# Who issues two small loads, who builds a table, and a new written order for all five queues

## The chip, the cores and the metric

One core of one Trainium2 chip runs the whole program. The metric is the device time of one execution in microseconds (us), given as the median over runs. A profile of one further execution supplies the rows that are quoted.

## The reference: what is computed

Sequence length S = 2048, width D = 448, hidden width F = 1792, all tensors bfloat16. Cut to what matters:

```python
def _A_ref(q, k, v, shift_k, ssm_k, ssm_D):      # q is layernorm(x)
    # k_shift[s] = sum over t of k[s-3+t] * shift_k[:, 3-t]      (4 taps per channel)
    kv = k_shift * v
    # y = causal convolution of kv with ssm_k, length 2048, per channel, by FFT of 4096 points
    y = y + kv * ssm_D
    return q * y

def _B_ref(x, w1, b1, w2, b2):                   # mixes tokens
    h = layernorm(x)
    u = gelu(einsum("bsd,sf->bdf", h, w1) + b1)
    return (einsum("bdf,fs->bds", u, w2) + b2) transposed to (b, s, d)

x = A_q
h = x + _A_ref(layernorm(x), A_k, A_v, A_shift_k, A_ssm_k, A_ssm_D)
h2 = h + _B_ref(layernorm(h), B_w1, B_b1, B_w2, B_b2)
```

## The kernel before

The 2048 positions are held as 128 partitions times R = 16 rows (position = 16 q + r). The long convolution is a transform built from matmuls in two stages, a product in the frequency domain, and two inverse stages. The program is a list of small operations, each with a step name "tag.number" and a position in that step, so `k2.5:4` is operation 4 of step 5 of tag k2. The tags, in the order of the data:

- `dummy`: a memset of a scratch tile by VectorE (L1061), a ScalarE activation that loads the GELU table (L1062), and nine matmuls on the scratch tile (L1071) that occupy TensorE until data is there.
- `con`: constants. `con.0` is the identity (L866, tensor c_id), `con.1` the first-stage table, `con.2` a compact second-stage table FC (c_fw, 258 KB). `con.3` to `con.6` spread FC into the full table FW, four operations on all of 1024 elements per partition (L881 on ScalarE, L882 on VectorE); every matmul of the second stage reads FW. `con.7` to `con.12` are later tables.
- `loads`: `loads.0` zeroes the fourth quarter of the filter tile KN (L903, VectorE); `loads.1` to `loads.4` load the four quarters of `ssm_k` (L906); `loads.5` loads the four taps `shift_k` in three pieces (L909 and two of L912); `loads.6, 7, 9, 11` are k and `loads.8, 10, 12, 13` v, in quarters of the rows; the rest are small vectors. The load of the fourth KN quarter, `loads.4`, has to wait for the memset `loads.0`.
- `kT`: transposes of the filter (L1083), evacuated to SBUF by ScalarE (L801) or VectorE (L804).
- `kv`: transposes of k (L986), a block of tap diagonals built by GpSimd (`kv.0`, L966 and L971), the four-tap convolution as matmuls (L1012), and the multiplication by v straight out of PSUM on VectorE (L1051).
- `k1` and `u1`: first transform stage of the filter and of kv (L1110, L1115), evacuated by either engine (L1126), then shuffled by DMA from SBUF to SBUF (L1130).
- `k2` and `u2`: second stage (L1150); the filter's is scaled on evacuation (L802, L805), the other copied (L801, L804).
- `i1`: 16 products in the frequency domain (L1176, 1792 elements per partition, all on VectorE), matmuls of the first inverse stage (L1195, 64 for each of eight groups), two evacuations for each group (L801) and two shuffling DMAs (L1210, L1215). `i1.4` is the group jj = 1, `i1.16` the group jj = 7.
- `q` and `xn`: layernorm statistics of x (L1252, L1254 on VectorE; the power on GpSimd, L1263) and normalised rows (L1285).
- `i2`: second inverse stage, row by row (L1316, L1321), gating by the normalised x (L1330, L1351, L1340), statistics of the result (L1357, L1369 and the small L1360, L1392) and the normalised row Q (L1402). `zero` is a GpSimd memset (L1161). `warm` are filler matmuls (L1226).
- `mlp`: the token MLP: 16 rows times 7 matmuls (L1449), 7 times 16 (L1459) with GELU, then 16 rows of output (L1470), each finished by VectorE (L1473) and stored.

Nothing is scheduled on the chip. The dictionary `ORDER` writes out, for each of the five queues (TensorE "pe", ScalarE "act", VectorE "dve", GpSimd "pool", SyncE "sp"), every operation in the order in which it is issued, and thereby also the engine of each operation that may run on more than one. A queue is strictly in order: an operation that waits holds back all that stand behind it. A planner in `schedule` walks these lists with estimated durations (`est`, `lat`, `rate`, `late`). It settles only which PSUM banks and buffers are taken, and so which waits are emitted. PSUM has eight banks; an evacuation of 896 elements frees a pair of them.

Apart from one output store on ScalarE's queue, all DMAs are issued by SyncE. The evacuations of k1, u1, k2, u2 and i1 alternate between ScalarE and VectorE as the lists say.

Of the kernel before, what the change touches and what calls it, by code (L numbers as in the profile page):

```python
# [33 lines left out]
    ),  # L34
    "act": (
# [9 lines left out]
    ),  # L45
    "dve": (
# [13 lines left out]
    ),  # L60
    "pool": (
        "kv.0:1-2 loads.14:0 q.0:0-1 kv.0:0 kv.0:3 q.1:4 q.2:4 q.1:5 q.2:5 xn.3:0 zero.0:0 xn.0:0 q.4:5 q.6:4-5 "
        "i2.7:0 i2.15:0 i2.27:0 i2.40:0 q.8:4-5 i2.53:0 i2.66:0 i2.79:0 i2.92:0 i2.105:0 i2.0:0 "
    ),
# [97 lines left out]
class _Sched:  # L162
# [50 lines left out]
    def op(self, W, fn, r=(), w=(), br=(), bw=(), n=0, kind=None, est=None, dmab=None, keng=16, rate=None, after=(), safter=(), mode=0, half=-1, late=0.0):  # L213
# [3 lines left out]
        o = _Op()  # L217
# [8 lines left out]
        if o.is_dma:  # L226
            o.est = {e: (585.0 if e == "pool" else 1400.0 if e == "act" else 700.0 if keng <= 8 else 460.0) for e in o.engs}
        elif est is not None:
            o.est = dict(est) if isinstance(est, dict) else {e: est for e in o.engs}
        else:  # L230
            o.est = {e: self.est_of(e, n, kind) for e in o.engs}
# [415 lines left out]
def _build(nc, A_q, A_k, A_v, A_shift_k, A_ssm_k, A_ssm_D, B_w1, B_b1, B_w2, B_b2, out):  # L647
# [5 lines left out]
    Bsz, S, D = A_q.shape  # L653
    F = B_w1.shape[1]
    assert Bsz == 1 and S == 2048 and D == 448 and F == 1792 and A_shift_k.shape[-1] == 4
    R = 16
    NFC = F // 128
    EPS = 1e-5
    DB = 2 * D

    bf16 = DT.bfloat16
    f16 = DT.float16
# [41 lines left out]
    with ctx:  # L704
# [107 lines left out]
        def emit_consts():  # L812
# [52 lines left out]
            def cload(o, src, n, dt=f16):  # L865
                op("sp", lambda e, W: e.dma_start(view(o, [n], dt), src), w=[(o, 2 * n)], dmab=128 * 2 * n)  # L866
            sch.t0 = -60.0
            cload(o_ID, d_id, 192, bf16)
            sch.t0 = -59.0
            cload(o_E0, d_e0, 256)  # L870
# [4 lines left out]
            for k in range(4):  # L875
                sch.t0 = -49.0 + k

                def spread(e, W, k=k):
                    dst = FW.rearrange("p t (c f v) -> p (t c) f v", c=2, f=4)[:, :, k, :]
                    if W == "act":  # L880
                        return e.activation(out=dst, in_=FC, func=ACT.Copy, scale=MK[:, k:k + 1])  # L881
                    return e.tensor_scalar(out=dst, in0=FC, scalar1=MK[:, k:k + 1], scalar2=None, op0=ALU.mult)  # L882
                op(FX, spread, r=[(o_FC, 2064)], w=[(o_FW, 8192, "fw")], n=1024, est={"act": 1150.0, "dve": 450.0})
# [16 lines left out]
        def emit_loads():  # L900
# [3 lines left out]
            for i, c in enumerate((0, 1, 2, 3)):  # L904
                sch.t0 = -20.0 + i
                op(Dq, lambda e, W, c=c: e.dma_start(KN[KP[c]:KP[c] + CW[c], c, :], A_ssm_k[128 * c:128 * c + CW[c], :]),  # L906
                   w=[(o_KN + 4096 * c, 4096)], dmab=CW[c] * 4096)
            sch.t0 = -15.0
            op(Dq, lambda e, W: e.dma_start(wsn[:, 0:3], A_shift_k[0:384].rearrange("(c p) j -> p c j", p=128)),  # L909
# [623 lines left out]
```

## Time and profile before

| | us |
|---|---|
| median of 3 runs (lowest, highest) | 172.03 (170.88, 172.7) |
| profiled execution, its own time | 171.0 |
| its span, first to last instruction | 169.2 |
| TensorE busy | 160.5 (95%) |
| VectorE busy | 94.5 (56%) |
| ScalarE busy | 88.1 (52%) |
| GpSimd busy | 17.4 (10%) |

The span is what the profile's rows are measured from; the profiled execution's own time is 1.8 us longer, and its rows are compared with that time, not with the median. A timeline row gives start and length in us, the engine, the line of the kernel, the tiles written and read, the count of merged instructions, and in brackets the idle time before them and what ended it. "PEld" is the weight load of TensorE, "SPq" SyncE issuing DMAs. An average over the whole span hides that the stages have different limits, so the windows are read stage by stage.

### The profile page before, as it was taken

The numbers are of one execution on the slowest core, as the hardware profiler recorded it, in microseconds if no ns is written. First come the engines' busy times: TensorE is split into PE (matmuls) and PEld (weight loads), VectorE is DVE, ScalarE is ACT, GpSimd is POOL, SyncE is SP. The second block draws the span as 40 slices with busy tenths as digits, with TensorE's granted clock in tenths as the row PEclk, the third lists the DMA queues.
The fourth block names the chain that finished last, engine by engine and source line by source line (L and its number), as shares of the span: only waits on it lengthen the run. The fifth ranks groups of instructions, "written<-read, shape, count | busy, mean of one in ns | idle before, by whom it ended". The sixth has DMA issues, their size and how long they took to land.

```text
span 169.2 us, 4200 instructions
## 1 busy us (share of the span) xinstructions
PE 160.5 (95%) x1821; PEld 99.8 (59%) x1821; DVE 94.5 (56%) x192; ACT 88.1 (52%) x133; POOL 17.4 (10%) x33
## 2 busy tenths in 40 slices
PE   4999999999988988999999999999999999999994
PEld 1677777433333766644555555555567777777784
DVE  3149889999999999999987710000003223132232
ACT  3389998899999688899777508311210000000000
POOL 1013000000421000054253210000000000000000
PEclk9999999999999999999999999999999999999999
DMA  4999959689939344575899999990000111101111
GB/s 135 344 344 405 412 224 350 244 262 338 414 113 341 125 164 172 219 267 182 288 398 403 410 421 418 417 406 16 0 4 0 54 54 54 54 4 54 54 54 54
DMA packets 16416, 36.69 MB, mean 217 GB/s; under 512 B 2253, under 2 KB 9934, under 8 KB 16398
## 3 DMA queue, kind: packets, MB, share of 16 engines
q1 hardware_dynamic: 16254, 36.34, 57.7%
q8 instruction: 14, 0.23, 0.5%
q10 hardware_dynamic: 144, 0.08, 0.2%
q14 instruction: 4, 0.03, 0.0%
HBM read 23.69 MB, written 1.84 MB: 151 GB/s over the span
## 4 chain that ended last, share of the span: by engine, by line
PE 75%; ACT 14%; DVE 4%; DMA 3%; SPq 1%; issue 1%; POOL 1%
PE ps L1470 25%; PE ps L1449 13%; PE ps L1459 13%; PE ps L1110 6%; ACT arena L801 6%; PE ps L1012 4%; ACT arena L1126 4%; PE ps L1150 4%; PE ps L1195 3%; ACT arena L802 3%; DMA arena<-in_A_ssm_k_dram 3%; PE ps L986 2%; PE ps L1316 2%; DVE arena L1252 2%; PE ps L1083 2%; DVE arena L1176 1%
## 5 line engine op out<-in xcount | busy, mean ns | idle before, releaser
L1473 DVE SCALAR_TENSOR_TENSOR arena<-ps,arena 128x448 bf16<-128x448 f32 (+2 forms) x17 | 11.2, 657 | 57.5 <-PE ps L1470 57.5
L1470 PE MATMUL ps<-arena 128*128 128x448 bf16 (+2 forms) x238 | 42.7, 342 | 0.0
L1470 PEld LDWEIGHTS ps<-arena 128*128 128x128 bf16 x238 | 33.2, 144 | 9.5
L801 ACT CAST arena<-ps 128x896 bf16<-128x896 f32 (+1 forms) x28 | 23.2, 883 | 4.9 <-PE ps L1195 3.8
L1126 ACT CAST arena<-ps 128x896 bf16<-128x896 f32 (+2 forms) x28 | 21.5, 815 | 1.9 <-PE ps L1110 0.9
L1449 PE MATMUL ps<-arena 128*128 128x448 bf16 x112 | 22.4, 353 | 0.0
L1459 PE MATMUL ps<-arena 128*128 128x448 bf16 x112 | 21.4, 352 | 0.0
L1439 ACT ACTIVATE arena<-ps,arena 128x448 bf16<-128x448 f32 x14 | 8.2, 640 | 20.6 <-PE ps L1459 14.7
L1195 PE MATMUL ps<-arena 64*32 64x448 bf16 x512 | 16.1, 350 | 1.3 <-ACT arena L801 1.3
L1449 PEld LDWEIGHTS ps<-arena 128*128 128x128 bf16 x112 | 10.9, 98 | 10.6 <-ACT arena L1330 0.6
L1176 DVE TENSOR_TENSOR arena<-arena 128x1792 bf16<-128x1792 bf16 x16 | 17.0, 1086 | 0.0
L1459 PEld LDWEIGHTS ps<-arena 128*128 128x128 bf16 x112 | 11.0, 98 | 10.2 <-ACT arena L1439 0.2
L1110 PE MATMUL ps<-arena 128*32 128x448 bf16 (+2 forms) x288 | 16.6, 335 | 0.4
L1150 PE MATMUL ps<-arena 128*64 128x448 bf16 x128 | 14.7, 359 | 1.8 <-ACT arena L801 1.2
L1195 PEld LDWEIGHTS ps<-arena 64*32 64x32 f16 x512 | 11.6, 90 | 5.8 <-ACT arena L801 3.2
L1150 PEld LDWEIGHTS ps<-arena 128*64 128x64 f16 x128 | 5.6, 108 | 10.5 <-ACT arena L801 3.3
L1110 PEld LDWEIGHTS ps<-arena 128*32 128x32 f16 x288 | 7.3, 95 | 5.9 <-ACT arena L802 2.1
L804 DVE COPY arena<-ps 128x1024 bf16<-128x1024 bf16 (+1 forms) x9 | 5.7, 658 | 7.8 <-PE ps L1083 7.4
L1051 DVE TENSOR_TENSOR arena<-ps,arena 128x512 bf16<-128x512 f32 (+1 forms) x16 | 9.0, 617 | 1.0 <-PE ps L1012 0.9
L1252 DVE BATCH_NORM_STATS2 arena<-arena 128x6 f32<-128x448 bf16 x16 | 9.4, 607 | 0.0
L805 DVE TENSOR_SCALAR arena<-ps 128x896 bf16<-128x896 f32 x8 | 8.5, 1087 | 0.9 <-PE ps L1150 0.8
L1330 ACT ACTIVATE arena<-ps,arena 128x448 f32<-128x448 f32 x11 | 7.7, 719 | 2.3 <-PE ps L1316 2.2
(63 smaller groups left out, 152.0 us busy)
## 6 DMA issues: line engine op xcount, KB each, us to landing
arena<-arena SPq DMA_DIRECT2D x16, 448.0 KB, 5.0
arena<-in_B_w_dram SPq DMA_DIRECT2D x8, 896.0 KB, 11.5
arena<-in_B_w_dram SPq DMA_DIRECT2D x2, 2048.0 KB, 17.0
arena<-arena SPq DMA_DIRECT2D x15, 224.0 KB, 2.3
arena<-in_B_w_dram SPq DMA_DIRECT2D x2, 1536.0 KB, 18.8
arena<-in_A_k_dram SPq DMA_DIRECT2D x4, 448.0 KB, 6.1
arena<-in_A_v_dram SPq DMA_DIRECT2D x4, 448.0 KB, 7.9
arena<-in_A_q_dram SPq DMA_DIRECT2D x4, 448.0 KB, 6.1
```

The costliest lines, as they stand in the source:

```text
L801: return e.copy(out=dst(), in_=src())
L1051: return e.tensor_tensor(out=v, in0=u.rearrange("p t (r d) -> p t r d", d=64), in1=v, op=ALU.mult)
L1110: op("pe", lambda e, W, quad=quad, r=r, q=q, x=x, c0=c0, d0=d0, dw=dw: e.matmul(quad(x, q), E0[:, 128 * x + c0:128 * x + c0 + 32], src[:, ...
L1126: return e.copy(out=dst, in_=u) if W == "act" else e.tensor_copy(out=dst, in_=u)
L1150: op("pe", lambda e, W, b=bs[h], h=h, j=j, c=c, par=par: e.matmul(PS[64 * par:64 * par + 64, b.slots[c], 0:D], FW[:, 2 * j + h, 64 * c:64 ...
L1176: op("dve", lambda e, W, m=m, i=i: e.tensor_tensor(out=MR(m.slots[0]).rearrange("p (x y) d -> p x y d", x=2), in0=TU[:, i].unsqueeze(2).br ...
L1195: k = op("pe", lambda e, W, bs=bs, m=ms[h], par=par, t=t, tab=tab, xy=xy, g=g, qd=qd: e.matmul(PS[32 * qd:32 * qd + 32, bs[g >> 1].slots[g ...
L1252: op("dve", lambda e, W, bs=bs, r=r: e.bn_stats(out=bs, in_=X[:, r, :]), r=[(o_X + r * DB, DB)], w=[(ob, 24)], n=D, kind="1x")
L1449: op("pe", lambda e, W, r=r, fc=fc, b=bs[fc]: e.matmul(Pb(b), W1A[:, r, 128 * fc:128 * fc + 128], Q[:, r, :], start=(r == 0), stop=(r == R ...
L1459: op("pe", lambda e, W, r=r, fc=fc, b=b: e.matmul(Pb(b), W1B[:, r, 128 * (fc - n0):128 * (fc - n0) + 128], Q[:, r, :], start=(r == 0), sto ...
L1470: op("pe", lambda e, W, r=r, fc=fc, b=b, d0=d0, d1=d1: e.matmul(Pb(b)[:, d0:d1], W2[fc // 7][:, fc % 7, r:S:R], G[:, fc, d0:d1], start=(fc ...
L1473: op("dve", lambda e, W, r=r, b=b, d0=d0, d1=d1: e.scalar_tensor_tensor(out=X[:, r, d0:d1], in0=Pb(b)[:, d0:d1], scalar=bm[:, r:r + 1], in ...
```

## The change

- The load of the identity (`con.0`) and one piece of the taps (`loads.5:1`) are issued from ScalarE's queue, ahead of and behind the GELU table load. The code now allows "sp" or "act" for all loads of `loads` and for the identity and first-stage table, with a planner estimate of 640 ns for an issue on ScalarE instead of 1400.
- Of the four spreads of the second-stage table, ScalarE keeps one; three go to GpSimd (before: three on ScalarE, one on VectorE).
- One of the 16 frequency products, `i1.1:0`, goes from VectorE to GpSimd.
- One of the 16 inverse-stage evacuations, `i1.4:64`, goes from ScalarE to VectorE.
- All five lists are written anew. VectorE clears the dummy tile before the KN quarter; SyncE loads the fourth KN quarter second; some u1 groups come earlier; VectorE has six u1 and six u2 evacuations instead of four and five, ScalarE nine of k2 instead of eight; two of the normalised rows `xn` come between ScalarE's i1 evacuations.
- A few planner estimates (`late`, the issue time 570 for 460) change; they reach the chip only through the waits that are emitted.

```diff
-            def cload(o, src, n, dt=f16):
-                op("sp", lambda e, W: e.dma_start(view(o, [n], dt), src), w=[(o, 2 * n)], dmab=128 * 2 * n)
+            def cload(o, src, n, dt=f16, W="sp", est=None):
+                op(W, lambda e, W: e.dma_start(view(o, [n], dt), src), w=[(o, 2 * n)], dmab=128 * 2 * n, est=est)
-            cload(o_ID, d_id, 192, bf16)
+            cload(o_ID, d_id, 192, bf16, ("sp", "act"))
-                op(FX, spread, r=[(o_FC, 2064)], w=[(o_FW, 8192, "fw")], n=1024, est={"act": 1150.0, "dve": 450.0})
+                op(("act", "dve", "pool"), spread, r=[(o_FC, 2064)], w=[(o_FW, 8192, "fw")], n=1024,
+                   est={"act": 1150.0, "dve": 450.0, "pool": 2850.0})
...
-                    op("dve", lambda e, W, m=m, i=i: e.tensor_tensor(
+                    op(("dve", "pool"), lambda e, W, m=m, i=i: e.tensor_tensor(
...
-                       r=[ru, (o_TK + i * 2 * DB, 2 * DB)], bw=[m], n=4 * D, after=aft, mode=1)
+                       r=[ru, (o_TK + i * 2 * DB, 2 * DB)], bw=[m], n=4 * D, after=aft, mode=1, est={"dve": 1005.0, "pool": 3450.0})
```

The heads of the new lists and the stretches that the steps below use:

```diff
 "act":
-"dummy.0:1 kT.2:8 kT.1:8 kT.5:8 kT.0:8 kT.6:8 k1.12:8 ...
+"con.0:0 dummy.0:1 loads.5:1 kT.3:8 kT.1:8 kT.7:8 kT.6:8 kT.4:8 k1.8:8 ...
-... i1.6:65-66 i1.4:64-65 i1.16:65 xn.1:0 i1.16:66 xn.5:0 xn.4:0 xn.2:0 i2.48:0 ...
+... i1.1:65-66 i1.14:65-66 xn.1:0 i1.8:66 ... i1.6:65 xn.2:0 i1.4:65 i1.16:65-66 xn.4:0 xn.5:0 i2.44:0 ...
 "dve":
-"loads.0:0 dummy.0:0 kT.3:8 ...
+"dummy.0:0 loads.0:0 kT.2:8 ...
+... kv.16:24-25 u1.9:8 k2.5:5 q.1:1 k2.9:4 q.1:3 u1.4:8 u1.11:8 u1.6:8 u1.7:8 k2.15:4 k2.3:4 k2.11:5 k2.1:4
+    u2.9:5 u2.13:5 k2.13:4 u2.1:5 i1.0:0 u2.5:5 q.4:0 u2.11:4 q.3:2 q.3:0 u2.15:4 i1.14:0 xn.0:1 i1.13:0 ...
+... i1.16:0 i1.15:0 q.5:2 q.4:2 i1.4:64 q.5:0 ... q.6:1 bias.0:1 i2.3:0 i2.11:0 i2.4:0 i2.12:0 i2.5:0 ...
 "pool":
-"kv.0:1-2 loads.14:0 q.0:0-1 kv.0:0 kv.0:3 q.1:4 q.2:4 q.1:5 q.2:5 xn.3:0 zero.0:0 xn.0:0 ...
+"loads.14:0 kv.0:0-1 q.0:0 kv.0:2-3 con.4:0 con.6:0 q.0:1 con.3:0 q.2:4-5 q.1:4-5 zero.0:0 xn.3:0 xn.0:0 i1.1:0 ...
 "sp":
-"loads.2:0 loads.5:2 con.0:0 loads.1:0 loads.3:0 loads.4:0 loads.9:0 loads.5:0 con.1:0 loads.6:0 loads.5:1 ...
+"loads.2:0 loads.4:0 loads.1:0 loads.3:0 loads.5:2 loads.11:0 con.1:0 loads.6:0 loads.5:0 loads.9:0 xload.0:0 loads.12:0 ...
+... i1.10:67 loads.15:0 i1.12:67 i1.6:67 i1.4:66-67 i1.16:67 i1.12:68 i1.16:68 i1.6:68 w1a.1:0 ...
```

More of the change, by code (lines that the diff above doesn't have):

```diff
@@ L14 @@
     "pe": (
[19 rows of a table removed]
[18 rows of a table added]
     ),
     "act": (
[9 rows of a table removed]
[9 rows of a table added]
     ),
     "dve": (
[13 rows of a table removed]
[13 rows of a table added]
     ),
     "pool": (
-        "kv.0:1-2 loads.14:0 q.0:0-1 kv.0:0 kv.0:3 q.1:4 q.2:4 q.1:5 q.2:5 xn.3:0 zero.0:0 xn.0:0 q.4:5 q.6:4-5 "
-        "i2.7:0 i2.15:0 i2.27:0 i2.40:0 q.8:4-5 i2.53:0 i2.66:0 i2.79:0 i2.92:0 i2.105:0 i2.0:0 "
+        "loads.14:0 kv.0:0-1 q.0:0 kv.0:2-3 con.4:0 con.6:0 q.0:1 con.3:0 q.2:4-5 q.1:4-5 zero.0:0 xn.3:0 xn.0:0 "
+        "i1.1:0 q.6:4 q.4:5 q.6:5 i2.7:0 i2.15:0 i2.27:0 i2.40:0 i2.53:0 i2.66:0 q.8:4-5 i2.79:0 i2.92:0 i2.105:0 "
+        "i2.0:0 "
     ),
     "sp": (
[6 rows of a table removed]
[6 rows of a table added]
         "mlp.31:15 mlp.33:15 mlp.35:15 mlp.37:15 mlp.38:15 mlp.39:31 "
@@ L226, in op @@
         if o.is_dma:
-            o.est = {e: (585.0 if e == "pool" else 1400.0 if e == "act" else 700.0 if keng <= 8 else 460.0) for e in o.engs}
+            o.est = {e: (585.0 if e == "pool" else 640.0 if e == "act" else 700.0 if keng <= 8 else 570.0) for e in o.engs}
         elif est is not None:
@@ L863, in emit_consts @@
             d_m, d_et, d_ew = const(c_m, "c_m"), const(c_et, "c_et"), const(c_ew.reshape(128, -1), "c_ew")
-            def cload(o, src, n, dt=f16):
-                op("sp", lambda e, W: e.dma_start(view(o, [n], dt), src), w=[(o, 2 * n)], dmab=128 * 2 * n)
+            def cload(o, src, n, dt=f16, W="sp", est=None):
+                op(W, lambda e, W: e.dma_start(view(o, [n], dt), src), w=[(o, 2 * n)], dmab=128 * 2 * n, est=est)
             sch.t0 = -60.0
-            cload(o_ID, d_id, 192, bf16)
+            cload(o_ID, d_id, 192, bf16, ("sp", "act"))
             sch.t0 = -59.0
-            cload(o_E0, d_e0, 256)
+            cload(o_E0, d_e0, 256, W=("sp", "act"))
             sch.t0 = -50.0
@@ L905, in emit_loads @@
                 sch.t0 = -20.0 + i
-                op(Dq, lambda e, W, c=c: e.dma_start(KN[KP[c]:KP[c] + CW[c], c, :], A_ssm_k[128 * c:128 * c + CW[c], :]),
+                op(("sp", "act"), lambda e, W, c=c: e.dma_start(KN[KP[c]:KP[c] + CW[c], c, :], A_ssm_k[128 * c:128 * c + CW[c], :]),
                    w=[(o_KN + 4096 * c, 4096)], dmab=CW[c] * 4096)
             sch.t0 = -15.0
-            op(Dq, lambda e, W: e.dma_start(wsn[:, 0:3], A_shift_k[0:384].rearrange("(c p) j -> p c j", p=128)),
+            op(("sp", "act"), lambda e, W: e.dma_start(wsn[:, 0:3], A_shift_k[0:384].rearrange("(c p) j -> p c j", p=128)),
                w=[(o_wsn, 24, "ws")], dmab=3072)
             for h in range(2):
-                op(Dq, lambda e, W, h=h: e.dma_start(wsn[64 * h:64 * h + 64, 3], A_shift_k[384:448]),
+                op(("sp", "act"), lambda e, W, h=h: e.dma_start(wsn[64 * h:64 * h + 64, 3], A_shift_k[384:448]),
                    w=[(o_wsn + 24, 8, "ws")], dmab=512)
@@ L923, in emit_loads @@
             op("pool", lambda e, W: e.memset(DR, 0.0), w=[(o_DR, DB)], est=400.0)
-            op(Dq, lambda e, W: e.dma_start(DR[0:1, :], A_ssm_D.rearrange("(a d) -> a d", a=1)),
+            op(("sp", "act"), lambda e, W: e.dma_start(DR[0:1, :], A_ssm_D.rearrange("(a d) -> a d", a=1)),
                w=[(o_DR, DB)], dmab=DB, keng=1)
             sch.t0 = -8.0
-            op(Dq, lambda e, W: e.dma_start(b1n[0:NFC, :], B_b1.rearrange("(c p) -> c p", p=128)), w=[(o_b1n, 256)],
+            op(("sp", "act"), lambda e, W: e.dma_start(b1n[0:NFC, :], B_b1.rearrange("(c p) -> c p", p=128)), w=[(o_b1n, 256)],
                dmab=F * 2, keng=14)
-            op(Dq, lambda e, W: e.dma_start(b2n, B_b2.rearrange("(q r) -> q r", r=R)), w=[(o_b2n, 32)], dmab=S * 2)
+            op(("sp", "act"), lambda e, W: e.dma_start(b2n, B_b2.rearrange("(q r) -> q r", r=R)), w=[(o_b2n, 32)], dmab=S * 2)
         def emit_xload():
@@ L1134, in emit_stage1 @@
                        br=[g], w=[(o_T + (4 * j + jh - 1) * 2 * DB, 4 * DB, tag) for j in range(4)],
-                       dmab=128 * 4 * DB, keng=16, rate=300.0, late=360.0 if i >= 2 else 0.0))
+                       dmab=128 * 4 * DB, keng=16, rate=300.0, late=250.0))
                 wbufs.append(g)
@@ L1217, in emit_products_i1 @@
                                r=[(o_u, 2 * DB)], w=[(o_z, 8 * DB, "z")],
-                               dmab=128 * 2 * DB, keng=16, rate=300.0, after=aft, late=300.0 if off >= 2 else 0.0)
+                               dmab=128 * 2 * DB, keng=16, rate=300.0, after=aft, late=300.0)
                     if jj == R // 2 - 1:
```

93 rows, old and new, of the table ORDER are left out of this document.

## The prediction

> **What bounds the kernel now.** I read the table of windows first, stage by stage, then the chain of work that ended last.
>
> ```profile
> core 0: us, PE busy (x) PEld busy (x) DVE busy (x) ACT busy (x) POOL busy (x), PEclk, DMA share, GB/s
> 4.30:11.30 7.00, 6.79 (x80) 5.47 (x78) 1.52 (x3) 4.03 (x5) 0.00 (x0) 1.00 0.98 340
> 11.30:31.70 20.40, 20.40 (x492) 15.09 (x490) 18.52 (x32) 18.64 (x25) 2.10 (x2) 1.00 0.86 327
> 31.70:54.20 22.50, 20.30 (x229) 7.49 (x225) 21.64 (x27) 21.46 (x26) 3.72 (x7) 1.00 0.84 295
> 79.50:103.00 23.50, 23.50 (x125) 11.97 (x124) 15.38 (x63) 14.10 (x36) 7.55 (x11) 1.00 1.02 387
> ```
>
> ```profile
> 7.17 1.21 PE ps L1083 x16
> ...
> 31.26 0.60 PE ps L1110 x8
> 31.86 0.02 issue
> 31.88 0.91 ACT arena L1126
> ...
> 124.37 42.51 PE ps L1470 x238
> ```
>
> The chain is TensorE without a break from 7.17 to 31.86, and its window is full (20.40 of 20.40). From 31.9 to 54 it alternates between evacuations and short TensorE pieces: VectorE (21.64 of 22.50) and ScalarE (21.46) are both full. From 79.5 to the end only matmuls remain and the change leaves their number alone. So the time is set by when the MLP starts, and that by three earlier stretches.
>
> **Part 1, start to first k1 matmul.**
>
> ```profile
> 1.00 0.91 DVE L903 MEMSET arena<- 128x1024 uint32 x1 [1.00 <-PEq L1518]
> 1.96 0.43 DVE L1061 MEMSET arena<- 128x448 bf16 x1
> 2.45 3.52 PE L1071 MATMUL ps<-arena 128*128 128x448 bf16 x9 [2.45 <-DVE arena L1061]
> 5.54 1.29 PEld L1083 LDWEIGHTS ps<-arena 128*128 128x128 bf16 x16 [0.35 <-DMA arena<-c_id]
> 5.78 1.18 PE L1083 MATMUL ps<-arena 128*128 128x128 bf16 x16
> 9.78 1.15 PE L1083 MATMUL ps<-arena 128*128 128x128 bf16 x16
> 11.31 1.32 PE L1110 MATMUL ps<-arena 128*32 128x448 bf16 x24
> ```
>
> ```profile
> L866 SPq DMA_DIRECT2D arena<-c_id x1: 575/575/575, 1.8 to 1.8; - x1
> DMA to landing us min/median/max: 3.7/3.7/3.7
> L906 SPq DMA_DIRECT2D arena<-in_A_ssm_k_dram x1: 584/584/584, 3.4 to 3.4; - x1
> DMA to landing us min/median/max: 5.6/5.6/5.6
> ```
>
> The identity lands at 1.8 + 3.7 = 5.5, but the nine dummy matmuls end only at 5.78: an earlier identity alone is worth nothing. What moves the start is the swap on VectorE: the dummy tile is clear at 1.00 + 0.43 = 1.43 instead of 2.39, the dummies end near 4.85, and the identity, issued by ScalarE from about 0.7, lands at 4.4. The transposes start at 4.9. The price of the swap is that the KN memset now ends at 1.5 + 0.91 = 2.4, and SyncE's second load waits for it; behind it stand all the others, the k quarters too. In the old order the third DMA was also issued near 2.4, so the same KN bytes are complete when they were before: 3.4 + 5.6 = 9.0, or 8.7 without identity and taps in the stream. The last pair of transposes starts at about 8.75 instead of 9.78, and after it and one group of kv the first k1 matmul stands at 10.65 instead of 11.31: -0.65. ScalarE's two issues (the SyncE rows take 0.57) lie in time when it is idle. Ends: 0 (the loads bound it) and -1.0.
>
> **Part 2, to the first k2 matmul** (31.68 before). TensorE's list up to there is the old one plus u1.2 and u1.3 and four more changes of tile shape. ScalarE loses two spreads (1.16 each), VectorE one (0.48), but the full engine here is TensorE, so I count nothing for it.
>
> ```profile
> 18.48 0.87 PE ps L1110 x16
> L881 ACT ACTIVATE arena<-arena 128x1024 f16<-128x1024 f16 x3 | 3.5, 1163 | 0.0
> L882 DVE TENSOR_SCALAR arena<-arena 128x1024 f16<-128x1024 f16 x1 | 0.5, 477 | 0.0
> L971 POOL TENSOR_TENSOR arena<-arena 128x1024 bf16<-128x1024 bf16 x1 | 1.9, 1906 | 0.1
> L1161 POOL MEMSET arena<- 128x1792 bf16 x1 | 1.6, 1592 | 3.5 <-DMA arena<-arena 3.5
> 31.68 0.95 PE L1150 MATMUL ps<-arena 128*64 128x448 bf16 x8
> ```
>
> Two u1 groups cost what two k1 groups do, 0.87 less a change of shape: 0.8. Four changes at 0.1 to 0.15: 0.5. First k2: 31.68 - 0.65 + 0.8 + 0.5 = 32.3.
>
> The three spreads on GpSimd must be done by then. No row shows one there: between 0.9 (the memset's 0.89 ns an element) and 3.8 (twice the tap block); I take 1.9, the tap block with as many elements. FC is now loaded after four KN and four k quarters, one of x and three of v: 5.7 MB by the sizes in the list of DMA issues, which at 340 GB/s after the first quarter's landing (4.3) is 19.7. Three times 1.9 ends at 25.4, three times 3.8 at 31.1, both before 32.3. They cost nothing unless one takes over 4.2.
>
> **Part 3, k2, u1, u2 up to the first i1 matmul**, S = 54.25.
>
> ```profile
> 33.51 2.56 ACT L1126 CAST arena<-ps 128x896 bf16<-128x896 f32 x3
> 46.49 3.09 DVE L804 CAST arena<-ps 128x896 bf16<-128x896 f32 x3
> 27.10 1.67 DVE L1252 BATCH_NORM_STATS2 arena<-arena 128x6 f32<-128x448 bf16 x3
> 54.11 7.27 DVE L1176 TENSOR_TENSOR arena<-arena 128x1792 bf16<-128x1792 bf16 x7
> 54.25 2.02 PE L1195 MATMUL ps<-arena 64*32 64x448 bf16 x64
> ```
>
> From start to start an evacuation takes ScalarE (2.56 - 0.91) / 2 = 0.82, VectorE (3.09 - 1.09) / 2 = 1.00, statistics 0.53, a product 1.03. By the new lists VectorE does, from u1.9 to u2.15:4, 18 evacuations, one product, three statistics and two small ones: 18.0 + 1.0 + 1.6 + 0.2 = 20.8. ScalarE does 23, 18.9. VectorE is the bound. It starts when kv.16 is multiplied, 32.0 (three u1 groups and a change of shape, 1.5, lie between its matmuls and k2; its multiplications then take 1.2). With 0.3 of gaps S becomes 53.1: -1.15. Ends: -2.0 (no change-of-shape cost, no gaps) and +0.2.
>
> The product on GpSimd: no row. VectorE's 1.08 below; at the tap block's 1.86 ns an element 3.3; twice that, 6.7, above. I take 3.3. It starts after `i1.0` (4.7 before S) and is needed 1.1 after S, so 5.8 of other work covers it.
>
> The Trainium skill's page SBUF — State Buffer (two separate sides) speaks against this: a VectorE instruction with two SBUF inputs and a GpSimd instruction that reads SBUF exclude each other for their whole length. The product pairs are of that kind, but in the new list the GpSimd one lies beside PSUM evacuations, so the sum is the same by it; no run here shows such a pair.
>
> **Part 4, i1 to the MLP.**
>
> ```profile
> 70.12 1.71 ACT L801 CAST arena<-ps 128x896 bf16<-128x896 f32 x2 [0.47 <-PE ps L1195]
> 72.31 0.91 ACT L801 CAST arena<-ps 128x896 bf16<-128x896 f32 x1 [0.47 <-PE ps L1226]
> 74.61 0.68 DVE L1351 SCALAR_TENSOR_TENSOR arena<-ps,arena 128x448 bf16<-128x448 f32 x1 [0.25 <-PE ps L1321]
> 78.87 0.39 DVE L1402 TENSOR_SCALAR arena<-arena 128x448 bf16<-128x448 bf16 x1
> 79.47 1.34 PE L1449 MATMUL ps<-arena 128*128 128x448 bf16 x6
> arena<-arena SPq DMA_DIRECT2D x15, 224.0 KB, 2.3
> ```
>
> i1 keeps its pace: group jj = 1 is complete at 70.12 = S + 15.9, the last at S + 18.1; the two `xn` between fill ScalarE's waits of 0.47. Now VectorE evacuates half of jj = 1, after all products and two statistics: S + 17.0. SyncE's list stands behind it; its DMA lands 2.3 later, S + 19.3. VectorE's own list (four statistics, nine small, 3.0) lets the first i2 combination start at S + 20.3, before at 74.61 = S + 20.4. From there to Q of row 0: two combinations 1.2, two statistics 1.1, three small 0.3, GpSimd's power 0.6, overlapped by two more combinations to 3.9, the normalisation 0.4, hand-over 0.1: 4.4. The MLP starts at S + 24.7, before 79.47 = S + 25.2. One more i2 row (0.38) now stands behind that start, and the next rows of Q come within 0.3 of their use: I add 0.3. Together +0.2.
>
> **Sum**: -1.15 + 0.2 = -0.95, say -1.0. The profiled execution took 171.0 (span 169.2 and 1.8 around it): 170.0. The median of the runs shown is 1.03 above that execution, so I state 171.0 against 172.03, its own range 169.9 to 172.2.
>
> **Rivals.**
> - *The freed engine time counts in full.* For: in 11.3 to 31.7 VectorE and ScalarE are over 90% busy too. Against: TensorE is at 100%. Then 2.3 + 0.5 of spreads and 1.0 of product over two engines give 1.9, with part 1 -2.55: 169.5.
> - *The start gives nothing*, because loads, not dummies, decide when k1 begins; ScalarE's issue then does nothing. 171.6.
> - *The hand-over eats the gain*, the slower side: VectorE, with 14 products in a row after S, paces the end of i1. At 1.09 each (as long as one runs) they end at S + 15.6, the evacuation at 17.8, the combination waits to S + 20.9, Q takes the 4.65 of before, the MLP starts at S + 25.7, and each late Q costs again, 0.9. With -1.15, +0.6: 172.6. It decides once the hand-over loses over 1.2.
> - *The table comes late*: a spread of 5.5 on GpSimd ends at 36.2, k2 and all u1 behind it in TensorE's queue wait 4: 175.
> - *The two kinds of product exclude each other*: if GpSimd's starts as late as S - 0.5, VectorE waits 2.8 for it: 173.8. The skill's rule above would do that.
>
> **How the numbers follow.** Forecast 0.39, freed time 0.20, empty start 0.06, hand-over 0.20, late table 0.10, exclusion 0.05. A measurement of this kernel tells about 1% (1.7 us) from no change. Faster by more: nearly all of the second case and a fifth of the first, 0.27. Slower by more: the late table, most of the exclusion and a fifth of the hand-over, 0.18. Within: 0.55. The range 169.0 to 173.9 leaves out the late table, half of the exclusion and the far end of the freed time.
>
> **What would show it.** First transposes at 4.9 and first k1 near 10.65; first k2 near 32.3; first i1 matmul near 53.1, released by VectorE; first MLP matmul near 77.8. A wait of L1150 on GpSimd would prove the late table, an idle TensorE before L1316 with VectorE full the hand-over; a k2 start before 31 would prove me wrong on part 2.

## Result and the profile after

The changed kernel takes 170.47 us (median of 22 runs, 170.06 to 171.07); the kernel before, in the same rounds, 171.26 (170.59 to 172.7). The ratio is 0.9951, 95% interval 0.9937 to 0.9966: 0.84 us faster, half a per cent. The profiled execution has a span of 168.4 instead of 169.2. Forecast was -1.0, so the sum is right. Its terms are not: the forecast put the gain ahead of the first i1 matmul, and it came behind it; the two errors cancel.

Two rows of the table of windows after, with columns as before:

```profile
11.30:31.70 20.40, 20.40 (x488) 15.19 (x484) 18.42 (x31) 15.88 (x23) 10.82 (x10) 1.00 0.91 338
31.70:54.20 22.50, 20.61 (x236) 7.18 (x236) 22.03 (x27) 21.80 (x27) 7.34 (x8) 1.00 0.91 302
```

From 11.3 to 31.7 ScalarE's busy time fell from 18.64 to 15.88 and GpSimd's rose from 2.10 to 10.82: the spreads have moved. TensorE is full there as before, so this time became idle time of ScalarE. From 31.7 to 54.2 VectorE and ScalarE are still both full.

The chain that ended last, start and length in us:

```profile
0.88 0.43 DVE arena L1062
...
1.48 0.92 DVE arena L904
...
2.42 0.66 SPq L907
...
3.12 4.63 DMA arena<-in_A_ssm_k_dram
...
7.80 1.21 PE ps L1084 x16
...
123.55 42.51 PE ps L1471 x238
```

It begins with VectorE's memset of the dummy tile (L1062), now first, and of the KN quarter (L904). Then come SyncE's load that waits for it and the KN load behind that one, for which the transposes wait. The chain of the kernel before also ran over a KN load:

```profile
2.42 4.71 DMA arena<-in_A_ssm_k_dram
```

So loads bound the start before and after, and the load that binds now comes 0.6 later (7.75 instead of 7.13), with 32 instead of 48 transposes behind it.

The marks that the prediction named, in the timelines of TensorE, VectorE and GpSimd (start, length, engine, line, tiles, count):

```profile
11.17 1.32 PE L1111 MATMUL ps<-arena 128*32 128x448 bf16 x24
...
32.66 1.57 PE L1151 MATMUL ps<-arena 128*64 128x448 bf16 x12
...
54.12 1.82 PE L1196 MATMUL ps<-arena 64*32 64x448 bf16 x64 [0.22 <-DVE arena L804]
...
78.32 1.34 PE L1450 MATMUL ps<-arena 128*128 128x448 bf16 x6
```

```profile
32.52 1.08 DVE L1127 CAST arena<-ps 128x896 bf16<-128x896 f32 x1
...
52.99 1.08 DVE L804 CAST arena<-ps 128x896 bf16<-128x896 f32 x1
...
69.79 1.09 DVE L804 CAST arena<-ps 128x896 bf16<-128x896 f32 x1
...
73.98 1.28 DVE L1352 SCALAR_TENSOR_TENSOR arena<-ps,arena 128x448 bf16<-128x448 f32 x2
...
77.78 0.39 DVE L1403 TENSOR_SCALAR arena<-arena 128x448 bf16<-128x448 bf16 x1
```

```profile
20.36 5.69 POOL L882 TENSOR_SCALAR arena<-arena 128x1024 f16<-128x1024 f16 x2 [5.99 <-DMA arena<-c_fw]
...
26.06 2.84 POOL L882 TENSOR_SCALAR arena<-arena 128x1024 f16<-128x1024 f16 x1
...
46.49 1.59 POOL L1162 MEMSET arena<- 128x1792 bf16 x1 [9.45 <-DMA arena<-arena]
...
49.57 3.58 POOL L1177 TENSOR_TENSOR arena<-arena 128x1792 bf16<-128x1792 bf16 x1 [1.18 <-DVE arena L1177]
```

Taken stage by stage, with the rows of before that the prediction shows (S is the first i1 matmul):

| stretch | before | predicted | measured |
|---|---|---|---|
| start to first k1 | 11.31 | -0.65 | -0.14 |
| first k1 to first k2 | 20.37 | +1.3 | +1.12 |
| first k2 to S | 22.57 | -1.8 | -1.11 |
| S to first MLP matmul | 25.22 | -0.5 | -1.02 |
| first MLP matmul to its last stage | 44.90 | +0.7 | +0.33 |
| sum | | -1.0 | -0.82 |

The first row is a single draw: in other executions with this start the first k1 comes up to 0.5 later (last section). One sum in the table stands out: from the first k1 to S it is 42.94 before and 42.95 after. The 1.12 more up to k2, where two u1 groups now stand ahead, and the 1.11 less from k2 to S cancel, so over that stretch nothing was gained. The gain is made behind S.

### The profile page after: what moved, and what is told of

Same layout as the page of the kernel before. It is cut to its first block, busy times and chain, and to the rows that moved or that the text cites. A ratio compares the mean times of both kernels' runs of the same rounds, so it can differ in the third digit from the quotient of the medians.

```text
span 168.4 us, 4214 instructions
## 1 busy us (share of the span) xinstructions
PE 160.9 (96%) x1821; PEld 99.8 (59%) x1821; DVE 95.7 (57%) x193; ACT 84.0 (50%) x128; POOL 29.1 (17%) x37
## 4 chain that ended last, share of the span: by engine, by line
PE 74%; DVE 13%; ACT 7%; DMA 3%; issue 1%; SPq 0%; DVEq 0%
PE ps L1471 25%; PE ps L1450 13%; PE ps L1460 13%; PE ps L1111 6%; ACT arena L801 5%; PE ps L1013 4%; PE ps L1317 4%; DVE arena L804 4%; DVE arena L1177 3%; DVE arena L805 3%; DMA arena<-in_A_ssm_k_dram 3%; PE ps L987 3%; PE ps L1196 2%; PE ps L1227 2%; PE ps L1084 1%; DVE arena L1253 1%
## 5 line engine op out<-in xcount | busy, mean ns | idle before, releaser
L801 ACT CAST arena<-ps 128x896 bf16<-128x896 f32 x25 | 21.4, 913 | 4.1 <-PE ps L1196 2.8
L1127 ACT CAST arena<-ps 128x896 bf16<-128x896 f32 (+2 forms) x27 | 20.1, 801 | 4.5 <-PE ps L1111 2.8
L1111 PE MATMUL ps<-arena 128*32 128x448 bf16 (+2 forms) x288 | 15.7, 335 | 0.3 <-ACT arena L1127 0.2
L1177 DVE TENSOR_TENSOR arena<-arena 128x1792 bf16<-128x1792 bf16 x15 | 15.8, 1090 | 0.0
L1196 PEld LDWEIGHTS ps<-arena 64*32 64x32 f16 x512 | 11.3, 90 | 6.2 <-ACT arena L801 2.5
L804 DVE COPY arena<-ps 128x1024 bf16<-128x1024 bf16 x9 | 6.1, 690 | 7.5 <-PE ps L1084 6.1
L1127 DVE CAST arena<-ps 128x896 bf16<-128x896 f32 x9 | 9.6, 1081 | 0.7 <-PE ps L1111 0.7
L882 POOL TENSOR_SCALAR arena<-arena 128x1024 f16<-128x1024 f16 x3 | 8.5, 2848 | 6.0 <-DMA arena<-c_fw 6.0
## 6 DMA issues: line engine op xcount, KB each, us to landing
arena<-in_B_w_dram SPq DMA_DIRECT2D x2, 2048.0 KB, 16.8
```

Source lines behind the costliest of these rows:

```text
L801: return e.copy(out=dst(), in_=src())
L804: return e.tensor_copy(out=dst(), in_=src())
L1111: op("pe", lambda e, W, quad=quad, r=r, q=q, x=x, c0=c0, d0=d0, dw=dw: e.matmul(quad(x, q), E0[:, 128 * x + c0:128 * x + c0 + 32], src[:, ...
L1127: return e.copy(out=dst, in_=u) if W == "act" else e.tensor_copy(out=dst, in_=u)
L1177: op(("dve", "pool"), lambda e, W, m=m, i=i: e.tensor_tensor(out=MR(m.slots[0]).rearrange("p (x y) d -> p x y d", x=2), in0=TU[:, i].unsqu ...
L1196: k = op("pe", lambda e, W, bs=bs, m=ms[h], par=par, t=t, tab=tab, xy=xy, g=g, qd=qd: e.matmul(PS[32 * qd:32 * qd + 32, bs[g >> 1].slots[g ...
```

## Experiments

Three theories stood against each other. A: the gain is made at the hand-over from i1 to the MLP, by one product fewer on VectorE. B: it comes from the earlier start and from the spreads taken off ScalarE and VectorE. C: only the new order matters, not which engine does what. All ratios are to the kernel before, with 95% intervals. Line numbers of the kernels below differ by up to two from those of the changed kernel.

### The product back on VectorE

```diff
 "dve":
-... u2.15:4 i1.14:0 xn.0:1 ...
+... u2.15:4 i1.1:0 i1.14:0 xn.0:1 ...
 "pool":
-... xn.3:0 xn.0:0 i1.1:0 q.6:4 ...
+... xn.3:0 xn.0:0 q.6:4 ...
```

> The changed kernel, but the product of the first i1 group (i1.1:0) is VectorE's again, right ahead of the next one. Theory A (the gain is made at the hand-over from i1 to the MLP, by one product fewer on VectorE): a product takes VectorE 1.0 from start to start, so the last product ends 1.0 later, at S + 15.6, the half of i1.4 on VectorE at S + 17.8, the first MLP matmul 0.7 to 1.0 later; about 171.3, ratio 0.999 to 1.001. Theory B (the gain comes from the earlier start and the spreads taken off ScalarE and VectorE) and theory C (only the new order matters, not who does what): no change from the changed kernel, 170.5, ratio 0.995.

Measured: 171.39, ratio 0.9994 (0.9975 to 1.0013). The whole gain is gone. First the timeline rows of this kernel, then what TensorE waited for in i1 (us in total, times, longest), before, after and here:

```profile
11.01 0.74 PE L985 MATMUL ps<-arena 128*128 128x128 bf16 x12 [0.34 <-DMA arena<-in_A_k_dram]
11.68 1.32 PE L1109 MATMUL ps<-arena 128*32 128x448 bf16 x24
...
54.63 1.57 PE L1194 MATMUL ps<-arena 64*32 64x448 bf16 x48 [0.23 <-DVE arena L802]
...
75.38 1.28 DVE L1350 SCALAR_TENSOR_TENSOR arena<-ps,arena 128x448 bf16<-128x448 f32 x2
...
79.72 1.34 PE L1448 MATMUL ps<-arena 128*128 128x448 bf16 x6
```

```profile
PE ps L1195 <- ACT arena L801: 1.3, 6, 0.2
```

```profile
PE ps L1196 <- ACT arena L801: 1.0, 4, 0.3
...
PE ps L1196 <- DVE arena L1177: 0.3, 1, 0.3
```

```profile
PE ps L1194 <- DVE arena L1175: 1.4, 2, 1.1
```

From k1 to S it is again 42.95 (54.63 - 11.68). From S to the MLP it is 25.09, against 24.20 with the product on GpSimd and 25.22 before. With 15 products behind S, VectorE paces i1 (1.4 of waits for L1175); with 14, ScalarE's evacuations do. The kernel before has 14 behind S too, and two ahead of it; the new list has one ahead, so that without GpSimd 15 are left. Theory A holds for the time; B and C said no change.

But the product is not the whole of the 1.02 gained between S and the MLP. VectorE's first i2 combination (74.61 before, 73.98 after, 75.38 here) stands at S + 20.36 before, S + 19.86 after and S + 20.75 here: 0.89 lie between the two kernels that differ in the product alone. From it to the first MLP matmul it is 4.86 before, 4.34 after and also 4.34 here: these 0.52 stay when the product is back, so they come from the rest of the change. The chain of the kernel before ran there over GpSimd's power, three normalised rows `xn` on ScalarE and the gating behind them:

```profile
73.33 1.00 POOL arena L1263
...
74.56 2.07 ACT arena L1285 x3
76.63 0.62 ACT arena L1330
```

In the changed kernel ScalarE does two of its four `xn` earlier, between the i1 evacuations, and the chain from 69.36 to the last stage is TensorE alone. That this move gives the 0.52 is likely, but it is not shown: no run moves the `xn` alone.

### The spreads back on ScalarE and VectorE

```diff
 "act":
-... con.5:0 k1.19:8 k1.1:10 k1.2:10 ...
+... con.5:0 k1.19:8 con.3:0 k1.1:10 con.4:0 k1.2:10 ...
 "dve":
-... kv.9:28-29 kv.10:24-25 ...
+... kv.9:28-29 con.6:0 kv.10:24-25 ...
 "pool":
-... kv.0:2-3 con.4:0 con.6:0 q.0:1 con.3:0 q.2:4-5 ...
+... kv.0:2-3 q.0:1 q.2:4-5 ...
```

> The changed kernel, but the three spreads of GpSimd are back on ScalarE (two) and VectorE (one), at places behind the landing of their table at 20.3. Theory A: TensorE is full up to the first k2 matmul and ScalarE has idle stretches of 1.2 there, so it costs 0 to 0.3: 170.5 to 170.8, ratio 0.995 to 0.997. Theory B: 2.3 of ScalarE and 0.5 of VectorE come back on two engines, 1.4: 171.9, ratio 1.003.

Measured: 170.95, ratio 0.996 (0.9936 to 0.9985), 0.15 above the changed kernel's. One row of this kernel's windows:

```profile
11.30:31.70 20.40, 20.19 (x476) 14.84 (x474) 18.20 (x30) 17.36 (x24) 2.27 (x6) 1.00 0.86 321
```

ScalarE has 17.36 of 20.40 busy and still room, as theory A says. In this one execution k1 to S is 43.41 (11.47 to 54.88), 0.46 more, of which TensorE's idle 0.21 is one part. The places of the three spreads are mine, and the times do not resolve so small a difference: the two intervals overlap. B's 1.4, a ratio of 1.003, lies outside.

### The half of i1.4 back on ScalarE

```diff
 "act":
-... xn.2:0 i1.4:65 i1.16:65-66 ...
+... xn.2:0 i1.4:64-65 i1.16:65-66 ...
 "dve":
-... q.4:2 i1.4:64 q.5:0 ...
+... q.4:2 q.5:0 ...
```

> The changed kernel, but the half of i1.4 that VectorE evacuates (i1.4:64) is ScalarE's again. ScalarE evacuates it at once when i1.4's matmuls end, near S + 16.9, so SyncE's transfer starts as before; VectorE's list ahead of the first i2 combination is 1.0 shorter, but i1.4's other half and i1.16's come 0.9 later from ScalarE. Theory A as it stands (what counts is the product, not who evacuates): within 0.3 of the changed kernel, 170.2 to 170.8. Rival (the evacuation on VectorE is itself part of the gain): the last i1 transfers and xn.4, xn.5 come 0.9 later and the MLP starts 0.5 to 0.9 later, 171.0 to 171.4.

Measured: 170.49, ratio 0.9947 (0.9924 to 0.997): no difference. VectorE's row ahead of the first i2 combination:

```profile
74.53 1.28 DVE L1352 SCALAR_TENSOR_TENSOR arena<-ps,arena 128x448 bf16<-128x448 f32 x2 [1.19 <-PE ps L1322]
```

VectorE now stands idle for 1.19 and the combination waits for TensorE's first i2 rows. In the changed kernel it began right behind VectorE's own list. Counted from S (54.63 here) it stands at S + 19.9 in both. So the two bounds of this place lie on each other: relief of VectorE beyond one product gives nothing there.

### The product alone, in the kernel before

```diff
 "dve":
-... u2.15:4 i1.13:0 u2.7:5 i1.1:0 i1.11:0 ...
+... u2.15:4 i1.13:0 u2.7:5 i1.11:0 ...
 "pool":
-... zero.0:0 xn.0:0 q.4:5 ...
+... zero.0:0 xn.0:0 i1.1:0 q.4:5 ...
```

> The kernel before, with one edit: product i1.1:0 is on GpSimd, behind the two small xn operations, and all else as it was. Theory A: VectorE's last product ends 1.0 earlier, the first MLP matmul 0.6 to 0.9 earlier: 170.4 to 170.7, ratio 0.995 to 0.997. Theory C: the product alone gives nothing without the new order: 171.3, ratio 1.000. A loss (ratio above 1.001) would mean that GpSimd's product comes too late for the first i1 matmuls or slows VectorE's beside it.

Measured: 172.54, ratio 1.0078 (1.0054 to 1.0101). My theory A said 170.4 to 170.7; it was wrong on this one. The timelines of VectorE and GpSimd show why:

```profile
52.14 3.81 DVE L1176 TENSOR_TENSOR arena<-arena 128x1792 bf16<-128x1792 bf16 x1
```

```profile
51.43 3.58 POOL L1176 TENSOR_TENSOR arena<-arena 128x1792 bf16<-128x1792 bf16 x1
```

GpSimd's product runs from 51.43 to 55.01. VectorE's next product, 1.08 long elsewhere, takes 3.81: it ends at 55.95, 0.94 behind GpSimd's. VectorE runs no other instruction in that time, and its next one starts at 55.88 instead of 53.11. With one product fewer on VectorE behind it, 1.3 of that is left at the first MLP matmul (80.74 instead of 79.47) and in the time. This is the rival of the two kinds of product, in a kernel in which they meet.

### Two products side by side, in the changed kernel

```diff
 "dve":
-... u2.5:5 q.4:0 u2.11:4 q.3:2 q.3:0 u2.15:4 i1.14:0 xn.0:1 i1.13:0 q.3:3 ...
+... u2.5:5 i1.13:0 q.4:0 u2.11:4 q.3:2 q.3:0 u2.15:4 i1.14:0 xn.0:1 q.3:3 ...
```

> The changed kernel, but VectorE does its product i1.13 at 50.4, ahead of four operations on PSUM and X, so that it lies beside GpSimd's product instead of behind it; the amount of work is the same. If the two kinds of product exclude each other: VectorE's takes until GpSimd's has ended at 53.15 and 0.95 more, 3.7 instead of 1.08; S comes 2.7 later with one product fewer behind it, 172.2 to 173.2, ratio 1.004 to 1.011. If the long product in the kernel before with GpSimd's product had another cause (its inputs came late there): each product keeps its 1.08 and 3.58, and only the order of VectorE's work differs, 170.3 to 171.2.

Measured: 173.13, ratio 1.0107 (1.0087 to 1.0128).

```profile
50.64 3.69 DVE L1176 TENSOR_TENSOR arena<-arena 128x1792 bf16<-128x1792 bf16 x1
```

```profile
49.80 3.58 POOL L1176 TENSOR_TENSOR arena<-arena 128x1792 bf16<-128x1792 bf16 x1 [1.17 <-DVE arena L1176]
```

The same product of VectorE goes from 1.08 to 3.69, again to 0.95 behind GpSimd's end (54.33 and 53.38), and the same work costs 2.7 more (1.0107 - 0.9951, times 171.3). Only the place of the product differs, so the exclusion is shown for this pair of instructions: VectorE's takes until GpSimd's has ended, while GpSimd's keeps its 3.58. The Trainium skill's page SBUF — State Buffer (two separate sides) states it: a VectorE instruction with two SBUF inputs and a GpSimd instruction that reads SBUF do not share, and the later one waits for the earlier to end. The two traces agree with it, and so do the rows of the changed kernel in which nothing is longer: beside GpSimd's product at 49.57 stand only evacuations from PSUM (the one at 52.99 has its 1.08) and statistics, which have one input.

### The early issue undone, and the whole start undone

The first kernel puts the identity and the late tap load back on SyncE; the second also puts VectorE's memset of KN ahead of the dummy tile again.

```diff
 "act":
-con.0:0 dummy.0:1 loads.5:1 kT.3:8 ...
+dummy.0:1 kT.3:8 ...
 "sp":
-loads.2:0 loads.4:0 loads.1:0 ... loads.9:0 xload.0:0 ...
+loads.2:0 con.0:0 loads.4:0 loads.1:0 ... loads.9:0 loads.5:1 xload.0:0 ...
 "dve":   (second kernel only)
-dummy.0:0 loads.0:0 kT.2:8 ...
+loads.0:0 dummy.0:0 kT.2:8 ...
```

> The changed kernel, but the identity and the late tap load are issued by SyncE again: the identity in the gap in which SyncE waits for VectorE's memset, the tap load behind eight of its loads. The identity lands 0.4 to 0.9 later. Theory A (the first k1 matmul waits for the KN and k loads, not for the identity): the transposes start at up to 5.5 instead of 4.77, but they wait for KN at 6.5 and 7.8 all the same; first k1 as before, time within 0.3 of the changed kernel, ratio 0.994 to 0.997. Theory B (the early identity is the gain): the whole row of work moves by 0.4 to 0.9, ratio 0.998 to 1.000.

> The changed kernel with its whole start undone: identity and late tap load on SyncE, and VectorE clears the KN rows ahead of the dummy tile. The dummies begin near 2.45 and end near 5.8 instead of 4.75; SyncE waits for the memset 0.5 less, so the KN loads land up to 0.5 earlier. Theory A (the start gives nothing to the end, since loads set the first k1 matmul): first k1 between 10.9 and 11.6, ratio 0.993 to 0.997. Theory B (the earlier dummies and identity are worth the 1.0 by which the transposes move): first k1 near 12, ratio 0.999 to 1.002. In between, ratio 0.997 to 0.999, if TensorE's half rate, which then lasts up to 1.1 longer after the start, falls into the transposes of some executions.

Measured: 170.37, ratio 0.9948 (0.993 to 0.9967), and 170.29, ratio 0.9942 (0.992 to 0.9964). The start gives nothing. TensorE's timelines of both:

```profile
11.31 0.94 PE L1110 MATMUL ps<-arena 128*32 128x448 bf16 x16
```

```profile
5.78 3.29 PE L1083 MATMUL ps<-arena 128*128 128x128 bf16 x48
...
11.13 1.32 PE L1110 MATMUL ps<-arena 128*32 128x448 bf16 x24
```

With dummies from 2.45, as before the change, and the new order of loads, k1 starts at 11.13, no later than the 11.17 of the changed kernel. There TensorE's transposes run without a wait; in the changed kernel they begin 1.0 earlier and wait for KN. Two bounds lie within 0.1 of each other in these two executions, and the swap on VectorE trades the one for the other.

### Whole KN quarters first, and the same without the inner dummies

Both edit the changed kernel. The first moves the KN quarter that waits for the memset behind the three others, and its transposes and their evacuations with it; the second also leaves out the three dummy matmuls between the transposes and puts the last transposes' evacuation on VectorE.

```diff
 "sp":
-loads.2:0 loads.4:0 loads.1:0 loads.3:0 loads.5:2 ...
+loads.2:0 loads.1:0 loads.3:0 loads.4:0 loads.5:2 ...
 "pe":
-... kT.3:0-7 kT.2:0-7 kT.6:0-7 kT.7:0-7 kT.1:0-7 kT.0:0-7 kT.1:9 kT.3:9 kT.5:0-7 kT.4:0-7 kT.5:9 ...
+... kT.3:0-7 kT.2:0-7 kT.1:0-7 kT.0:0-7 kT.1:9 kT.3:9 kT.5:0-7 kT.4:0-7 kT.5:9 kT.6:0-7 kT.7:0-7 ...
# second kernel: kT.1:9 kT.3:9 kT.5:9 left out (N_WK = 0), and kT.7:8 from "act" to "dve"
```

> The changed kernel, but SyncE issues the three whole KN quarters ahead of the half one that waits for VectorE's memset, and TensorE transposes the half one last. Theory A (the start is bound by the loads, and these stand behind a SyncE that waits for the memset from 1.1 to 2.4): the stream of loads starts 1.3 earlier, the k quarter lands 1.0 to 1.3 earlier, the first k1 matmul comes near 10.0 to 10.4, and since TensorE is full from there on, all of it reaches the end: 169.3 to 169.8, ratio 0.988 to 0.991. Rival (what is gained at the start is lost again before S, where v, x and the table land and VectorE and ScalarE are full): within 0.3 of the changed kernel, ratio 0.993 to 0.997.

> e6_kn_order again, for one more profile. If the time at which TensorE's transposes change from 0.107 to 0.062 from start to start differs between executions of the same kernel (it was 7.3 in the first), it will most likely be earlier here, between 4 and 6.5; the row of transposes is then up to 1.0 shorter, the first k1 matmul waits for the k quarter at 9.7 and stands near 10.7 to 11.0. If the late change belongs to the kernel, it is at 7.3 again and the first k1 at 11.4.

Measured: 170.36, ratio 0.9937 (0.9916 to 0.9958), one more execution 170.06. I had expected 169.3 to 169.8. TensorE's timelines in the first and the second execution of this kernel:

```profile
4.75 2.74 PE L1084 MATMUL ps<-arena 128*128 128x128 bf16 x24
...
9.38 1.16 PE L1084 MATMUL ps<-arena 128*128 128x128 bf16 x16
10.38 0.73 PE L987 MATMUL ps<-arena 128*128 128x128 bf16 x12
11.44 1.32 PE L1111 MATMUL ps<-arena 128*32 128x448 bf16 x24 [0.33 <-ACT arena L801]
```

```profile
4.71 2.69 PE L1084 MATMUL ps<-arena 128*128 128x128 bf16 x29
...
11.03 1.32 PE L1111 MATMUL ps<-arena 128*32 128x448 bf16 x24 [0.33 <-ACT arena L801]
```

The first rows of the two are read up to the same time, 7.2, and hold 24 and 29 transposes. In the first execution a transpose takes 0.107 from start to start there (2.45 over 23 steps) and 0.062 later (1.00 over 16, from 9.38 to 10.38); 28 steps in at most 2.49 are about 17 long ones and 11 short ones, so in the second the change comes near 6.5. With the loads earlier, TensorE's own row of transposes, and behind it ScalarE's evacuation, took their place as the bound, with a length that differs from one execution to the next.

> The kernel of e6_kn_order, without the three dummy matmuls that stand between the transposes (0.19 to 0.37 each), and with the last evacuation of the transposes on VectorE instead of ScalarE. In e6 TensorE went without a break from 4.75 to 11.4, and 24 of its transposes took 0.107 from start to start instead of 0.062. Theory A, as e6 amends it (once the loads come earlier, TensorE's own row of transposes, at its half rate up to 5 to 7.3, and the waits for their evacuation set the first k1 matmul): 0.6 to 0.9 shorter there, first k1 near 10.5 whatever the time of the change of rate, 169.4 to 169.9, ratio 0.989 to 0.992. Rival (what is gained at the start is lost before S): first k2 less than 0.3 earlier than in e6, ratio 0.993 to 0.995.

Measured: 169.51, ratio 0.9904 (0.9867 to 0.9941), 0.8 faster than the changed kernel by the ratios, whose intervals just touch; span 167.7. TensorE's timeline:

```profile
4.71 4.51 PE L1084 MATMUL ps<-arena 128*128 128x128 bf16 x64
9.70 0.74 PE L987 MATMUL ps<-arena 128*128 128x128 bf16 x12 [0.49 <-DMA arena<-in_A_k_dram]
10.37 1.32 PE L1111 MATMUL ps<-arena 128*32 128x448 bf16 x24
...
53.32 1.82 PE L1196 MATMUL ps<-arena 64*32 64x448 bf16 x64 [0.22 <-DVE arena L804]
...
77.66 1.34 PE L1450 MATMUL ps<-arena 128*128 128x448 bf16 x6
```

k1 stands at 10.37, S at 53.32: again 42.95 between them. All 0.80 of the start reach S and 0.66 reach the MLP. So a gain at the start does pay; the change only did not make one. Of the three things relieved here, only the order of the loads was also tried by itself, and alone it gave nothing. In the row at 9.70 TensorE now waits for the k quarter. Its landing, from the chain of this kernel and then from issue and time to landing in the changed kernel:

```profile
3.74 5.92 DMA arena<-in_A_k_dram
```

```profile
L918 SPq DMA_DIRECT2D arena<-in_A_k_dram x1: 587/587/587, 4.8 to 4.8; - x1
...
DMA to landing us min/median/max: 5.7/5.7/5.7
```

It lands at 9.7 here and at 10.5 there: 0.8 earlier, which is what k1 gained.

## Why the prediction was right, and where it was wrong

**Right for the sum, by luck.** The forecast put -1.15 ahead of S and +0.2 behind it. Measured are -0.13 ahead of S and -0.69 behind it: two errors of 1.0 and 0.9 that cancel.

**Part 1: the step that failed** is that the last pair of transposes starts at about 8.75 and the first k1 matmul at 10.65. The step ahead of it held: the last KN quarter lands at 9.0 (issued at 3.7, landing 5.3 later), as before (3.4 + 5.6). What was left out is what comes ahead of and behind that quarter. With the fourth quarter second in SyncE's list, its wait for the memset holds up two more KN quarters. The first of them lands at 7.75 (3.12 + 4.63) instead of 7.13, and 1.4 of transposes and dummies lie between it and the last pair, which starts at 9.2. (It was the fourth load, not the third, that the old list issued near 2.4.) And the k quarter, which I named but gave no time, lands at 10.5 instead of 10.1. The first kv group needs it and takes 0.67, so k1 could not stand ahead of 11.17 in this execution. In three others with the same start TensorE waits for that quarter (0.34, 0.39 and 0.91). The rival "the start gives nothing" had it right. With the early dummies and the early issue undone the kernel is as fast.

**Part 2: near.** +1.12 for the two u1 groups and the changes of shape, where I had 1.3. A spread on GpSimd takes 2.85, not the 1.9 taken from the tap block; the bounds, 0.9 and 3.8, hold it, and the planner's estimate in the diff, 2850 ns, would have been the better source. The table's load landed at 20.3 (I had 19.7), the spreads ended at 28.90, 3.8 ahead of the first k2 matmul. The late table did not come.

**Part 3: a term mis-sized by 0.45.** That VectorE is the bound and releases S is right. From u1.9's evacuation to the release it took 21.55 (32.52 to 52.99 + 1.08) where I had 21.1; the other half of the 1.0 by which S is late is part 1's, since VectorE began at 32.52, not at 32.0, with k1 late by 0.5. GpSimd's product took 3.58 (I had 3.3) and was done 0.97 ahead of S.

**Part 4: too cautious.** The last half evacuation ends at S + 16.8 (I had 17.0), the combination starts at S + 19.9 (20.3), the Q row takes 4.2 (4.4, and 4.65 before; it stays short when the product is back), and the stalls for which I added 0.3 are absent; the extra i2 row costs its 0.33. The rival in which VectorE paces i1 needed 15 products behind S to come true: with the product back it did, 25.09 from S to the MLP, against that rival's 25.7.

**The exclusion rival** was priced at 2.8 for a product that starts late; 2.73 and 2.61 were measured where the products met. In the changed kernel they don't. The doubt was about where GpSimd's product would stand, and there the order kept it apart.

**Product and order belong together.** Without the product the rest of the change gives nothing (0.9994): the 0.52 that it saves ahead of the MLP goes into a 15th product behind S. The product alone loses (1.0078); together 0.9951. The order holds the stretch free of products beside GpSimd's. It also lets GpSimd begin in time: the clearing of the zero tile, which stands ahead of the product in its list and waits for a transfer, was here before

```profile
49.69 1.59 POOL L1161 MEMSET arena<- 128x1792 bf16 x1 [3.49 <-DMA arena<-arena]
```

and now stands at 46.49. Which of the moves in VectorE's list are needed for this was not taken apart.

## What to carry to other kernels

Work given to a slower engine pays only where the engine that gives it up is the pace-maker behind that point, and where its neighbours in time are of a kind that does not exclude it: look at the operands of what runs beside it, not at the engine's idle share. Where two bounds lie close together, taking away one shows nothing; the start became faster only when loads, dummies and an evacuation were relieved together. A load that waits for a memset holds up the loads behind it in its queue: 1.3 us on SyncE here. And a forecast is checked term by term: a sum that comes out right can hide two wrong stages.

## What the hardware showed that was not expected

TensorE's slow phase at the start ends at a time of its own. In two executions of one kernel (whole KN quarters first) the transposes went from 0.107 to 0.062 near 7.3 and near 6.5. The granted clock of the profile shows nothing of it. The windows of the first execution, the second of them from the change on:

```profile
4.75:7.30 2.55, 2.55 (x25) 2.55 (x25) 0.61 (x1) 1.01 (x1) 0.00 (x0) 1.00 0.92 341
7.30:7.80 0.50, 0.50 (x10) 0.50 (x9) 0.08 (x1) 0.27 (x1) 0.00 (x0) 1.00 0.48 161
```

PEclk is 1.00 in both, with 25 transposes in 2.55 and 10 in 0.50. The Trainium skill's page TensorE: Matmul & The Clock Gate (Part 1: The HAM clock gate) describes a half rate until about 3.4 us of activity have passed in a window that runs free of the kernel, with the change varying by 500 ns either way. The dummy matmuls agree with a half rate (0.37 from start to start at first, 0.19 between the transposes later); the transposes less so, with 0.107 against 0.062. The change came later than that here, 5.1 and 5.9 behind the first matmul at 1.4. So a single profile of the first 12 us is one draw, the more as landings move too: in five executions with the start of the changed kernel, its own and four of the kernels above, the first k1 stood between 11.17 and 11.68, and its own was the earliest.
